# Windowed attention plus a gated FFN on one core: moving one weight load to the sync queue and adding window sums in three steps

## The chip, the core and the metric

The kernel runs on one core of a Trainium2 chip. The core has a matrix engine (TensorE, PE in the profile), a vector engine (VectorE, DVE), a scalar engine (ScalarE, ACT), GpSimd (POOL), and SyncE (SP), which here only issues transfers. Transfers run on 16 DMA engines; those issued by SyncE go through hardware queue q1, those issued by GpSimd through software queue q0. The metric is the device time of one execution in microseconds; less is better.

## The reference

One layer norm feeds an attention over a dilated window and a gated feed-forward network; both results are added to the input. The shapes are: 2048 tokens, 640 features, 32 heads of 20 features, a window of 8 positions that are 2 apart, 1536 hidden features, all in bf16.

```python
def _A_ref(x, wqkv, wo):                       # H = 32, W, dil = 8, 2
    q, k, v = ...                              # x @ wqkv, split into heads
    idx = pos[:, None] - (jnp.arange(W) * dil)[None, :]
    kg, vg = k[:, :, idx_c, :], v[:, :, idx_c, :]
    logits = jnp.einsum("bhsd,bhswd->bhsw", q, kg) * scale
    logits = jnp.where(mask[None, None, :, :], logits, -1e9)   # idx >= 0
    attn = _softmax(logits, axis=-1)           # over the 8 slots of the window
    o = jnp.einsum("bhsw,bhswd->bhsd", attn, vg)
    return o.transpose(...) @ wo
def _B_ref(x, w_gate, w_up, w_down):
    return ((x @ w_gate) * (x @ w_up)) @ w_down

xn = _layernorm(x, axis=-1)
return x + _A_ref(xn, A_wqkv, A_wo) + _B_ref(xn, B_w_gate, B_w_up, B_w_down)
```

## The kernel before

The 2048 tokens are four chunks (`c` = 0 to 3) of 512, and each chunk is four tiles (`ttl`) of 128; `tg` counts the sixteen tiles. A chunk goes through these stages.

- `norm(c, ...)`: VectorE takes the statistics of each tile (`stats`), GpSimd the reciprocal root, VectorE scales (`xn`). For chunk 0 TensorE transposes the tiles. For the later chunks `keep` (line 294) stores the four tiles to `xnD` in DRAM and `turn_all` (line 302) loads them back transposed into `xnT`, both on the sync queue. For those chunks the tile `xn` lies in the buffer ring `pw` of six buffers, which the products of the logits use too, so a product may have to wait until the store of `xn` is through.
- `vproj(c)` and `qk(c)`: projections on TensorE; ScalarE copies them out of PSUM. The values go to DRAM (`vD`), on the sync queue for chunk 0 and on GpSimd's for the others.
- `weights(c)` (line 424): eight products `pw` of `qT` with a shifted `kT` on VectorE, one for each slot of the window. Each group of four is followed by `heads`, 20 matmuls with the constant `Ek` that add up the 20 features of each head (`lps`), and by an exponential on ScalarE into `e`.
- `turned_weights(c)` (line 462): `keep_e` stores `e` to `eD`, and `turn_e` loads it transposed as `eT`, both on the sync queue.
- `attend(c, ttls)` (line 490): once per chunk `normal`, planned as `("a", c)`, which adds up the 8 slots of every head, takes the reciprocal and scales `eT`. Then for each tile, on VectorE: `mix` (the gathered values `v8` times the weights) and three halving additions (`add4`, `add2`, `add1`); the result is stored to `oD` and loaded transposed as `oT`. `v8` has two buffers; the load of the tile after next is issued when a tile is done.
- `glu(c)` (line 558): gate and up matmuls (`psg`, `psu`), copied out by ScalarE, multiplied by VectorE into `hT`.
- `finish(c)` (line 591): for each tile and each half of the output columns 5 matmuls with `wo_perm` and 12 with `wd` into `psf`, then on VectorE the addition of the input tile `xr`, then the store. For a chunk's first tile the last 4 of the 12 come in a unit of their own, since the last `hT` come late.

The weights are loaded once. `load_down` (line 158) loads the output weights `wo_perm` (four DMAs of 200 KB) and the down weights `wd` (one of 1920 KB); `load_ffn` loads gate and up weights (four DMAs of 960 KB). Both are issued on GpSimd's queue, `load_down` behind `load_ffn` and the constants.

The order in which each engine gets its instructions is written out by a small planner when the program is built (`run`, line 197). It keeps a clock for TensorE and one for VectorE, in microseconds of its own. An operation (`op`) has a planned cost and a time from which it may start. At each step the engine that is behind takes an operation: first one from its list of interludes (`burst` for TensorE, which holds `heads`; `quick` for VectorE, which holds `hT`, the mask and the residuals), if one is due, otherwise the next one of its main line (`main` for TensorE, `chain` for VectorE). Entries in `later`, most of them DMA issues, are put out as soon as the slower of the two clocks has reached their due time. What the planner reckons decides only the order on each engine. On the chip each instruction waits for its operands, and an engine never passes an instruction that waits.

In this plan `turn_e` falls due 3.0 after `keep_e`, `eT` counts as there 7.0 after `turn_e`, and `normal` costs 2.8. `heads` counts as ready 0.9 after its fourth product has been planned to end (`LAG` 0.2 and a slack of 0.7). VectorE's chain from line 652 on is: norms of chunks 0 and 1, `weights(0)`, norm of chunk 2, all four tiles of `attend(0)`, `weights(1)`, norm of chunk 3, tiles 4 and 5, `weights(2)`, tiles 6 to 9, `weights(3)`, the rest. TensorE's main line is at lines 678 to 693.

Of the kernel before, what the change touches and what calls it, by code (L numbers as in the profile page):

```python
# [10 lines left out]
F32 = dt.float32  # L11
# [6 lines left out]
def kernel(  # L18
# [139 lines left out]
    def load_down():  # L158
        wo_r = A_wo.rearrange("(h t jl) d -> jl h t d", h=H, t=KT, jl=JL)
        for jl in range(JL):  # L160
            nc.gpsimd.dma_start(out=wo_perm[jl * H : (jl + 1) * H, :, :], in_=wo_r[jl])
        nc.gpsimd.dma_start(out=wd[:], in_=B_w_down.rearrange("(f p) d -> p f d", p=P))

    def warm_up(n):
        wps = ps_log.tile([P, CS], F32, name="wps", tag="lg")
# [60 lines left out]
    def norm(c, group):  # L226
        st = state[c]
        st["xnT"] = None

        def alloc():  # L230
            if st["xnT"] is None:
                st["xnT"] = cpool.tile([P, KT, CS], BF, name="xnT", bufs=3)

        def steps(t0):
            g = {}

            def stats():
                g["mv"] = cpool.tile([P, group, nc.vector.BN_AGGR_DIM], F32, name="mv", bufs=2)
                for k in range(group):
                    x_t = x_tiles[c * CH + t0 + k]  # L240
                    s = cpool.tile([P, 2, nc.vector.BN_STATS_DIM], F32, name="stats")
                    for hf in range(2):
                        nc.vector.bn_stats(s[:, hf, :], x_t[:, hf * N2 : (hf + 1) * N2])  # L243
                    nc.vector.bn_aggr(g["mv"][:, k, :], s[:])
                rstd = cpool.tile([P, group], F32, name="rstd", bufs=2)
                g["rstd"] = rstd
                if c == 0 and t0 < 2:
                    nc.scalar.activation(rstd[:], g["mv"][:, :, 1], ACT.Sqrt, bias=eps[:])
                    return
                nc.gpsimd.tensor_scalar(rstd[:], g["mv"][:, :, 1], EPS, None, op0=ALU.add)  # L250
                nc.gpsimd.tensor_tensor(
                    rstd[:], rstd[:], mhalf[:].to_broadcast([P, group]), ALU.pow
                )

            def stats_after(t):
                if c == 0 and t0 < 2:
                    on("act", ("rstd", c, t0), t + LAG, 0.25)
                    return
                on("pool", ("rstd", c, t0), t + LAG, 0.85)

            op(chain, ("stats", c, t0), stats, 1.12 * group, None, stats_after)

            def scaling(ttl, k):
                def scale_x():
                    if c == 0 and t0 < 2:
                        nc.vector.reciprocal(g["rstd"][:], g["rstd"][:])
                    if c < 1:
                        xn_t = apool.tile([P, D], BF, name="xn_t", tag="o16")
                    else:
                        if ttl == 0:  # L270
                            st["xn"] = apool.tile([P, CH, D], BF, name="xn", tag="pw", bufs=6)
                        xn_t = st["xn"][:, ttl, :]
                    nc.vector.tensor_scalar(
                        xn_t[:], x_tiles[c * CH + ttl][:],
                        scalar1=g["mv"][:, k, 0:1], scalar2=g["rstd"][:, k : k + 1],
                        op0=ALU.subtract, op1=ALU.mult,
                    )
                    st["xn", ttl] = xn_t

                def turn():  # L280
                    alloc()
                    pst = ps_tr.tile([P, KT, P], BF, name="pst", tag="tr")
                    for i in range(KT):
                        nc.tensor.transpose(
                            pst[:, i, :], st["xn", ttl][:, i * P : (i + 1) * P], ident[:]
                        )
                    nc.scalar.copy(st["xnT"][:, :, tcols(ttl)], pst[:])
                    if c == ttl == 0:
                        warm_up(14)

                def turned(t):
                    on("act", ("xnT", c, ttl), t + LAG, 0.7)

                def keep():
                    nc.sync.dma_start(
                        out=xnD[c * CS : (c + 1) * CS, :].rearrange("(t p) d -> p t d", p=P),
                        in_=st["xn"][:],
                    )
                    done["kept", c] = min(clock["pe"], clock["dve"])
                    later.append((turn_all, lambda t=clock["dve"]: t + 4.0))  # L300

                def turn_all():
                    alloc()
                    nc.sync.dma_start_transpose(
                        out=st["xnT"][:],
                        in_=xnD[c * CS : (c + 1) * CS, :].rearrange("m (k p) -> m k p", p=P),
                    )
                    done["stored", c] = min(clock["pe"], clock["dve"])
                    done["turned", c] = min(clock["pe"], clock["dve"])
                    for k in range(CH):  # L310
                        done["xnT", c, k] = done["turned", c] + 8.0

                def scaled(t):
                    if c >= 1:
                        if ttl == CH - 1:
                            later.append((keep, lambda t=t: t))
                        return
                    op(burst, ("turn", c, ttl), turn, 0.3, when(("xn", c, ttl)), turned,
                       ("tr", ("xnT", c, ttl)), 0.7)

                def later_free():
                    old = done.get(("turn", c, ttl - 2), INF) if c < 1 else 0.0
                    return max(done.get(("rstd", c, t0), INF), old if ttl >= 2 else 0.0)

                op(chain, ("xn", c, ttl), scale_x, 0.43 if c or t0 >= 2 else 0.53, later_free, scaled,
                   ("pw", ("stored", c)) if c >= 1 and ttl == 0 else None)

            return [lambda k=k: scaling(t0 + k, k) for k in range(group)]

        if group == 1:  # L330
            for pair in ((0, 1), (2, 3)):
                for f in [steps(t0)[0] for t0 in pair]:
                    f()
        else:
            for t0 in range(0, CH, group):
                for f in steps(t0):
                    f()
# [124 lines left out]
    def turned_weights(c):  # L462
        st = state[c]

        def mask():
            nc.vector.tensor_tensor(
                st["e"][:, :, 0:MC], st["e"][:, :, 0:MC], vmask[:], ALU.mult
            )

        def keep_e():  # L470
            rows = eD[c * 2 * P : (c + 1) * 2 * P, :]
            nc.sync.dma_start(out=rows.rearrange("(g p) t -> p g t", p=P), in_=st["e"][:])
            later.append((turn_e, lambda t=min(clock["pe"], clock["dve"]): t + 3.0))

        def turn_e():
            st["eT"] = apool.tile([P, CH, 2 * P], BF, name="eT")
            rows = eD[c * 2 * P : (c + 1) * 2 * P, :]
            nc.sync.dma_start_transpose(
                out=st["eT"][:], in_=rows.rearrange("r (t p) -> r t p", p=P)
            )  # L480
            done["turned e", c] = min(clock["pe"], clock["dve"])
            done["eT", c] = done["turned e", c] + 7.0

        exps = when(("exp", c, 0), ("exp", c, 1))
        if c == 0:
            op(quick, ("mask", c), mask, 0.1, exps)
            exps = when(("mask", c))
        later.append((keep_e, exps))

    def attend(c, ttls):  # L490
        st = state[c]

        def normal():
            eT = st["eT"][:].rearrange("p t (w h) -> p t w h", h=H)
            rs = apool.tile([P, CH, H], F32, name="rs", bufs=1)
            nc.vector.tensor_reduce(
                rs[:], eT.rearrange("p t w h -> p t h w"), axis=AX.X, op=ALU.add
            )
            nc.vector.reciprocal(rs[:], rs[:])
            nc.vector.tensor_tensor(  # L500
                eT, eT, rs[:, :, None, :].to_broadcast([P, CH, W, H]), ALU.mult
            )

        if ttls[0] == 0:
            op(chain, ("a", c), normal, 2.8, when(("eT", c)))
        for ttl in ttls:
            tg = c * CH + ttl

# [140 lines left out]
    def side(fn):  # L649
        op(chain, ("side", len(chain)), fn, 0.0)  # L650
# [2 lines left out]
    side(load_ffn)  # L653
    norm(1, 4)
    side(constants)
    side(load_down)
    later.append((lambda: load_x(2), when(("v", 0, CH - 1, 1))))
    later.append((lambda: want_v8(0), when(("kept", 1))))
    weights(0)
# [5 lines left out]
    weights(1)  # L665
    turned_weights(1)
    norm(3, 4)
    attend(1, range(2))
    weights(2)
    turned_weights(2)  # L670
    attend(1, range(2, CH))
    attend(2, range(2))
    weights(3)
    turned_weights(3)
    attend(2, range(2, CH))
    attend(3, range(CH))

    vproj(0, range(CH))
# [46 lines left out]
```

## Time and profile before

| | |
|---|---|
| median of 6 runs | 275.41 us |
| lowest and highest run | 273.15 and 280.26 us |
| the profiled execution | 273.56 us, its span 271.6 us |
| DMA in the span | 52.18 MB, mean 192 GB/s |
| share of the 16 DMA engines | q1 52.9%, q0 14.0% |
| chain that ended last | PE 59%, DVE 19%, DMA 15% of the span |
| largest groups on VectorE | `pw` 32 products 46.3 us; `hT` 48 products 19.8 us |

The span runs from the first to the last instruction of the profiled execution, and its own time is 2.0 us longer. Busy times of matmuls are modelled and pipelined, so a row's length holds a little of the next row; starts are the better guide. In the rows of the timelines the columns are start, length, engine, line, operation, output and inputs, size and count, and in brackets the idle time before and what ended it. Rows of "SPq" are DMAs at the time they are issued; a DMA lands later. DMAs on the sync queue are issued in program order, and one that waits holds up those behind it.

### The profile page before, as it was taken

What the parts mean: (1) busy time and instruction counts of PE and PEld (TensorE: products, weight loads), DVE (VectorE), ACT (ScalarE), POOL (GpSimd) and SP (SyncE); (2) the same over time, 40 slices, a digit from 0 to 9 for tenths busy, and PEclk for the clock granted to TensorE, in tenths of its full rate; (3) what the DMA queues carried; (4) which work ended last, traced back from release to release, by engine and by line L of the source; (5) the groups of instructions that cost most, each with busy time, mean ns of one, the idle gap of its engine ahead of it and who ended that gap; (6) DMA issues with size and microseconds to landing.
All of it is one profiled execution on the core that took longest, in us unless ns stands there. A gap on an engine that the chain in (4) does not pass through costs nothing.

```text
span 271.6 us, 4138 instructions
## 1 busy us (share of the span) xinstructions
PE 261.5 (96%) x1607; PEld 144.7 (53%) x1624; DVE 202.1 (74%) x260; ACT 104.1 (38%) x185; POOL 39.2 (14%) x81
## 2 busy tenths in 40 slices
PE   7799999999999799999999999999999999999994
PEld 7554443445546367644444677744446774445773
DVE  4453969479689995499999857999999989821221
ACT  3655564555556000155555610054551005554000
POOL 1528201000302204100000131220000302000100
PEclk9999999999999899999999999999999999999998
DMA  6999999692999935705920998597188499210111
GB/s 187 306 381 389 317 364 189 179 264 53 262 315 295 335 99 150 213 32 161 276 46 2 272 312 174 188 271 171 39 228 250 119 292 283 81 47 2 48 48 48
DMA packets 53554, 52.18 MB, mean 192 GB/s; under 512 B 24754, under 2 KB 50816, under 8 KB 53536
## 3 DMA queue, kind: packets, MB, share of 16 engines
q1 hardware_dynamic: 49920, 38.48, 52.9%
q0 software_dynamic: 3616, 13.46, 14.0%
q8 instruction: 12, 0.20, 0.3%
q14 instruction: 6, 0.05, 0.1%
HBM read 35.39 MB, written 10.90 MB: 170 GB/s over the span
## 4 chain that ended last, share of the span: by engine, by line
PE 59%; DVE 19%; DMA 15%; issue 3%; SPq 1%; POOL 1%; ACT 0%; DVEq 0%; ACTq 0%
PE psu L567 15%; PE psg L567 15%; PE psf L616 14%; PE psf L609 6%; DMA xnD<-xn 5%; DVE pw L432 5%; DMA x_t<-in_A_x_dram 4%; PE psqk L360 4%; PE lps L443 3%; DMA v_929<-vD 3%; DMA xr<-in_A_x_dram 2%; PE psv L386 2%; DVE stats L243 1%; DVE v_407 L511 1%; DVE v_929 L511 1%
## 5 line engine op out<-in xcount | busy, mean ns | idle before, releaser
L567 PE MATMUL psu<-xnT,wu 128*128 128x512 bf16 x240 | 59.7, 379 | 0.0
L567 PE MATMUL psg<-xnT,wg 128*128 128x512 bf16 x228 | 59.0, 379 | 0.6
L616 PE MATMUL psf<-wd,hT 128*128 128x320 bf16 x384 | 57.9, 301 | 0.0
L572 ACT CAST gs<-psg 128x512 bf16<-128x512 f32 x48 | 28.1, 586 | 70.0 <-PE psg L567 50.9
L432 DVE TENSOR_TENSOR pw<-qT,kT 128x2560 bf16<-128x2560 bf16 x32 | 46.3, 1484 | 6.2 <-ACT kT L366 3.7
L616 PEld LDWEIGHTS <-hT 128*128 128x128 bf16 x384 | 37.8, 99 | 15.1 <-DVE hT L577 0.2
L360 PE MATMUL psqk<-xnT,wqkv 128*128 128x512 bf16 x195 | 43.9, 379 | 0.3
L567 PEld LDWEIGHTS <-wu 128*128 128x128 bf16 x240 | 23.3, 98 | 28.7 <-issue 0.8
L567 PEld LDWEIGHTS <-wg 128*128 128x128 bf16 x240 | 23.3, 98 | 28.2 <-issue 0.8
L572 ACT CAST us<-psu 128x512 bf16<-128x512 f32 x48 | 28.1, 586 | 26.1 <-PE psu L567 26.1
L623 DVE TENSOR_TENSOR osb<-psf,xr 128x320 bf16<-128x320 f32 x32 | 15.3, 486 | 25.2 <-PE psf L616 19.3
L577 DVE TENSOR_TENSOR hT<-gs,us 128x512 bf16<-128x512 bf16 x48 | 19.8, 418 | 16.5 <-ACT us L572 16.2
L360 PEld LDWEIGHTS <-wqkv 128*128 128x128 bf16 x200 | 19.4, 98 | 23.7 <-issue 0.8
L609 PE MATMUL psf<-wo_perm,oT 128*128 128x320 bf16 x160 | 27.6, 304 | 0.0
L386 PE MATMUL psv<-wqkv,xnT 128*128 128x320 bf16 x160 | 22.7, 299 | 0.0
L633 POOL DMA_DIRECT2D out_dram<-osb x13 | 7.1, 546 | 102.7 <-DVE osb L623 102.6
L609 PEld LDWEIGHTS <-oT 128*128 128x128 bf16 x160 | 15.7, 99 | 7.7 <-issue 1.3
L243 DVE BATCH_NORM_STATS2 stats<-x_t 128x6 f32<-128x320 bf16 x32 | 13.6, 466 | 7.6 <-DMA x_t<-in_A_x_dram 7.6
L386 PEld LDWEIGHTS <-xnT 128*128 128x128 bf16 x160 | 15.5, 98 | 6.3
L398 POOL DMA_DIRECT2D vD<-v_t x12 | 6.6, 552 | 79.1 <-ACT v_t L392 79.1
L392 ACT CAST v_t<-psv 128x320 bf16<-128x320 f32 x32 | 13.6, 426 | 6.9 <-PE psv L386 6.5
L366 ACT CAST qT<-psqk 128x512 bf16<-128x512 f32 x20 | 11.7, 586 | 10.1 <-PE psqk L360 10.1
(94 smaller groups left out, 194.6 us busy)
## 6 DMA issues: line engine op xcount, KB each, us to landing
x_t<-in_A_x_dram SPq DMA_DIRECT2D x16, 160.0 KB, 5.7
xr<-in_A_x_dram POOLq DMA_DIRECT2D x16, 160.0 KB, 3.9
out_dram<-osb POOLq DMA_DIRECT2D x13, 160.0 KB, 2.8
wg<-in_B_w_gate_dram POOLq DMA_DIRECT2D x2, 960.0 KB, 11.1
wu<-in_B_w_up_dram POOLq DMA_DIRECT2D x2, 960.0 KB, 13.3
xnD<-xn SPq DMA_DIRECT2D x3, 640.0 KB, 3.6
wd<-in_B_w_down_dram POOLq DMA_DIRECT2D x1, 1920.0 KB, 14.9
vD<-v_t POOLq DMA_DIRECT2D x12, 160.0 KB, 4.9
```

Of the source, the lines that this page charges most:

```text
L243: nc.vector.bn_stats(s[:, hf, :], x_t[:, hf * N2 : (hf + 1) * N2])
L360: nc.tensor.matmul(ps[:], lhsT=wqkv[:, i, r * D + j * P : r * D + (j + 1) * P], rhs=st["xnT"][:, i, :], start=(i == 0), stop=(i == KT - 1),)
L366: nc.scalar.copy(dst[:, j, o : o + CS], ps[:])
L386: nc.tensor.matmul(ps[:, 0:N2], lhsT=st["xnT"][:, i, tcols(ttl)], rhs=wqkv[:, i, 2 * D + n0 : 2 * D + n0 + N2], start=(i == 0), stop=(i == ...
L392: nc.scalar.copy(v_t[:].rearrange("p (j h) -> p j h", j=Dh)[:, :, k * HH : (k + 1) * HH], ps[:, 0:N2].rearrange("p (h j) -> p j h", j=Dh),)
L432: nc.vector.tensor_tensor(pt[:], st["qT"][:], st["kT"][:, :, off : off + CS], ALU.mult)
L567: nc.tensor.matmul(ps[:], lhsT=w[:, i, f * P : (f + 1) * P], rhs=st["xnT"][:, i, :], start=(i == 0), stop=(i == KT - 1),)
L572: nc.scalar.copy(s[:], ps[:])
L577: nc.vector.tensor_tensor(h[:], st["gu", 0, f][:], st["gu", 1, f][:], ALU.mult)
L609: nc.tensor.matmul(ps[:, 0:N2], lhsT=st["oT", ttl][:, i, :], rhs=wo_perm[:, i, n0 : n0 + N2], start=(i == 0), stop=False,)
L616: nc.tensor.matmul(ps[:, 0:N2], lhsT=st["hT", f][:, tcols(ttl)], rhs=wd[:, f, n0 : n0 + N2], start=False, stop=(f == FT - 1),)
L623: nc.vector.tensor_tensor(osb[:, n0 : n0 + N2], ps[:, 0:N2], xr[:, n0 : n0 + N2], ALU.add)
```

## The change

`load_down` is issued on the sync queue instead of GpSimd's, right behind the transposing load of chunk 1 (in `turn_all`, when `c == 1`), and no longer from VectorE's planned chain. In `normal` the reduction over the slots becomes three additions in f32 over halves: 8 slots to 4, 4 to 2, 2 to 1. Their scratch tile `s4` takes the single buffer of `e`. The planner's figures change: `turn_e` falls due 2.2 after `keep_e`, `eT` counts as there 7.5 after `turn_e`, `normal` costs 3.4. And one tile of `attend(1)` and one of `attend(2)` move behind the next chunk's `weights`.

```diff
     def load_down():
         wo_r = A_wo.rearrange("(h t jl) d -> jl h t d", h=H, t=KT, jl=JL)
         for jl in range(JL):
-            nc.gpsimd.dma_start(out=wo_perm[jl * H : (jl + 1) * H, :, :], in_=wo_r[jl])
-        nc.gpsimd.dma_start(out=wd[:], in_=B_w_down.rearrange("(f p) d -> p f d", p=P))
+            nc.sync.dma_start(out=wo_perm[jl * H : (jl + 1) * H, :, :], in_=wo_r[jl])
+        nc.sync.dma_start(out=wd[:], in_=B_w_down.rearrange("(f p) d -> p f d", p=P))
...
                     done["stored", c] = min(clock["pe"], clock["dve"])
+                    if c == 1:
+                        load_down()
                     done["turned", c] = min(clock["pe"], clock["dve"])
...
-            later.append((turn_e, lambda t=min(clock["pe"], clock["dve"]): t + 3.0))
+            later.append((turn_e, lambda t=min(clock["pe"], clock["dve"]): t + 2.2))
...
-            done["eT", c] = done["turned e", c] + 7.0
+            done["eT", c] = done["turned e", c] + 7.5
...
             rs = apool.tile([P, CH, H], F32, name="rs", bufs=1)
-            nc.vector.tensor_reduce(
-                rs[:], eT.rearrange("p t w h -> p t h w"), axis=AX.X, op=ALU.add
+            s4 = apool.tile([P, CH, 4, H], F32, name="s4", tag="e", bufs=1)
+            nc.vector.tensor_tensor(s4[:], eT[:, :, 0:4, :], eT[:, :, 4:8, :], ALU.add)
+            nc.vector.tensor_tensor(
+                s4[:, :, 0:2, :], s4[:, :, 0:2, :], s4[:, :, 2:4, :], ALU.add
             )
+            nc.vector.tensor_tensor(rs[:], s4[:, :, 0, :], s4[:, :, 1, :], ALU.add)
...
-            op(chain, ("a", c), normal, 2.8, when(("eT", c)))
+            op(chain, ("a", c), normal, 3.4, when(("eT", c)))
...
-    side(load_down)
...
-    attend(1, range(2))
+    attend(1, range(1))
     weights(2)
     turned_weights(2)
-    attend(1, range(2, CH))
-    attend(2, range(2))
+    attend(1, range(1, CH))
+    attend(2, range(1))
     weights(3)
     turned_weights(3)
-    attend(2, range(2, CH))
+    attend(2, range(1, CH))
     attend(3, range(CH))
```

## The prediction

> **What bounds the kernel now.** I read the page first, then the waits, then TensorE in order of time, then the granted clock, and last VectorE and the queues where TensorE had waited.
>
> ```profile
> span 271.6 us, 4138 instructions
> PE 261.5 (96%) x1607; PEld 144.7 (53%) x1624; DVE 202.1 (74%) x260; ACT 104.1 (38%) x185; POOL 39.2 (14%) x81
> PEclk9999999999999899999999999999999999999998
> ```
>
> TensorE is the bound: 271.6 - 261.5 leaves 10.1 us without a matmul, most of it before the weights arrive and after the last matmul. What can be won inside is small, and it lies where TensorE waits for VectorE or runs at a lower clock (the lone 8 in PEclk).
>
> ```profile
> PE lps L443 <- DVE pw L432: 2.4, 3, 1.0
> ```
> ```profile
> 42.00 1.24 PE L443 MATMUL lps<-pw,Ek 128*32 128x512 bf16 x17 [0.49 <-DVE pw L432]
> ```
> ```profile
> 87.50 0.84 PE L609 MATMUL psf<-wo_perm,oT 128*128 128x320 bf16 x5
> 88.18 1.25 PE L616 MATMUL psf<-wd,hT 128*128 128x320 bf16 x8
> 89.36 0.39 PE L443 MATMUL lps<-pw,Ek 128*32 128x512 bf16 x2
> 90.60 0.38 PE L443 MATMUL lps<-pw,Ek 128*32 128x512 bf16 x1 [0.85 <-DVE pw L432]
> 92.00 1.75 PE L443 MATMUL lps<-pw,Ek 128*32 128x512 bf16 x17 [1.03 <-DVE pw L432]
> ...
> 97.67 0.84 PE L609 MATMUL psf<-wo_perm,oT 128*128 128x320 bf16 x5
> ...
> 100.07 1.26 PE L443 MATMUL lps<-pw,Ek 128*32 128x512 bf16 x20
> ```
> ```profile
> 92.00:93.00 1.00, 1.00 (x16) 0.79 1.07 385
> ...
> 95.00:96.00 1.00, 1.00 (x5) 0.50 1.01 335
> ```
>
> The expensive place is the logits of chunk 1, `heads(1,0)`: TensorE arrives at 89.36, three of its 20 matmuls can run, and the fourth waits for the fourth `pw` product until 92.00. Then the clock is at 0.50 for the 3.4 us from about 92.8 (the columns are busy time, clock, DMA). The wait costs some 2.5 us, the half clock half of 3.4, so 1.7: 4.2 us in one place. A lesser stall, 0.49 us, stands at 42.00.
>
> **Part 1, the load moved.** On GpSimd's queue `load_down` sits behind the gate and up weights:
>
> ```profile
> 25.23 2.34 POOL L161 DMA_DIRECT2D wo_perm<-in_A_wo_dram  x4
> 27.56 1.07 POOL L162 DMA_DIRECT2D wd<-in_B_w_down_dram  x1
> 46.39 0.28 POOL L250 TENSOR_SCALAR rstd<-mv 128x4 f32<-128x4 f32 x1 [17.77 <-DVE mv L244]
> ```
> ```profile
> 22.83 0.40 SPq L295 DMA_DIRECT2D xnD<-xn  x1
> 30.06 0.38 SPq L412 DMA_DIRECT2D v_407<-vD  x1
> 37.23 7.89 SPq L304 DMA_TRANSPOSE xnT<-xnD  x1
> 46.69 0.38 SPq L472 DMA_DIRECT2D eD<-e  x1
> 49.83 0.38 SPq L295 DMA_DIRECT2D xnD<-xn  x1
> 50.30 1.90 SPq L478 DMA_TRANSPOSE eT<-eD  x1
> ```
> ```profile
> q0 software_dynamic: 965, 3.93, 68.7%
> ```
> ```profile
> q0 software_dynamic: 393, 1.57, 89.6%
> q1 hardware_dynamic: 209, 0.26, 14.2%
> ```
> ```profile
> 33.33 1.48 DVE L432 TENSOR_TENSOR pw<-qT,kT 128x2560 bf16<-128x2560 bf16 x1
> 37.31 1.49 DVE L432 TENSOR_TENSOR pw<-qT,kT 128x2560 bf16<-128x2560 bf16 x1 [2.50 <-DMA xnD<-xn]
> ```
>
> By 29 us q0 has moved 3.93 MB (window 14 to 29), just the four 960 KB gate and up loads; so from 29 on its traffic is this load alone. From 30 to 36 it leaves sync's queue 0.26 MB, and chunk 1's `xnD` store, issued at 22.83, lands only at 37.2, where its transpose starts. That store holds a `pw` buffer, and VectorE stands 2.50 us for it.
>
> Without the load, the some 0.34 MB still missing at 30 (0.26, and a little to 37.2) go at the rate of sync's queue alone:
>
> ```profile
> DMA packets 2030, 2.36 MB, mean 295 GB/s; under 512 B 187, under 2 KB 2030, under 8 KB 2030
> ```
>
> (window 4 to 12). That is 1.2 us: landing near 31.2, bounds 30 and 37.2. The 2.50 us wait goes; its product ran 37.31 to 38.7 and the two after it to 41.9, all now 2.5 earlier, ahead of TensorE's arrival at 41.12. Gain on TensorE 0.49 us, bounds 0 and 0.49.
>
> The price is the new place. Five issues at 0.4 us are 2 us on SP; POOL is freed 3.4 us, worth nothing, as it idles until 46.39. Behind them on SP and in its ring is `e`'s store (46.69). In ring order, at 295 GB/s: `v_407` (1.31 MB, 4.4 us) to 35.6, the transpose (0.66 MB, 2.2) to 37.8, wo and wd (4 x 200 + 1920 KB = 2.79 MB, 9.4) to 47.2.
>
> ```profile
> eD<-e SPq DMA_DIRECT2D x1, 256.0 KB, 2.1
> eT<-eD SPq DMA_TRANSPOSE x1, 4.2
> ```
>
> The `e` store then lands near 49.3 instead of 48.8, and `eT` near 53.5. Its user `a(0)` stands behind the last `hT` (below), so 2.3 us of cover are left. The weights themselves are wanted at 87.50: 40 us of cover.
>
> **Part 2, three additions for the reduction.**
>
> ```profile
> 55.92 0.42 DVE L577 TENSOR_TENSOR hT<-gs,us 128x512 bf16<-128x512 bf16 x1 [1.64 <-ACT us L572]
> 56.27 1.88 DVE L496 TENSOR_REDUCE rs<-eT 128x128 f32<-128x1024 bf16 x1
> ...
> 60.42 2.83 DVE L511 TENSOR_TENSOR v_407<-v_407,eT 128x5120 bf16<-128x5120 bf16 x1
> ...
> 74.13 2.83 DVE L511 TENSOR_TENSOR v_855<-v_855,eT 128x5120 bf16<-128x5120 bf16 x1 [2.32 <-DMA v_855<-vD]
> ...
> 86.26 11.30 DVE L432 TENSOR_TENSOR pw<-qT,kT 128x2560 bf16<-128x2560 bf16 x8
> ```
> ```profile
> 46.50 0.17 DVE L466 TENSOR_TENSOR e<-e,vmask 128x32 bf16<-128x32 bf16 x1
> ```
> ```profile
> L623 DVE TENSOR_TENSOR osb<-psf,xr 128x320 bf16<-128x320 f32 x32 | 15.3, 486 | 25.2 <-PE psf L616 19.3
> ```
>
> Removed: 1.88 us. Added: 512, 256 and 128 elements, f32 out. Bounds: at the reduction's own 1.83 ns an element, 896 elements make 1.64 us; at the rate of the all-bf16 `hT` (0.42 for 512, then about 0.27 and 0.2) 0.9 us. The nearest row with an f32 operand is `osb`: 486 ns for 320. With some 0.14 us fixed (the 32-element row takes 0.17) that is 1.08 ns an element, and 0.69 + 0.42 + 0.28 = 1.39, with two more gaps of 0.03: 0.43 saved per chunk, bounds 0.2 and 0.95. All of it lies in VectorE's chain `a(0)`, four tiles, `pw(1,..)`. `s4` takes the slot of `e`: it waits for the `e` store, which `eT` already awaited, and the next `e` waits for additions that stand ahead of its own `pw` products on VectorE: nothing.
>
> `a(0)` starts when the last `hT` of chunk 0 is done, paced by TensorE: 56.27 - 0.49. The chain is then 0.49 + 0.43 = 0.92 earlier, if `v_855`'s load (a 2.32 us wait) shifts along, as it starts when the first tile's buffer is free. Fourth `pw`: 86.26 + 4 x 1.41 = 91.9, now 91.0. Eighth: 97.6, now 96.6.
>
> **Part 3, the planner's figures.** They move instructions and cost none. Following its clock through the code, `turn_e` falls due at 45.16 + 2.2 and goes out at 47.65 instead of 48.47, ahead of chunk 2's `xnD` store on SP, no longer behind it (49.83 before 50.30). `eT` counts as there at 55.15 (55.47 before), `a(0)` takes 3.4 for 2.8, so the chain is planned 0.30 later. `heads(1,0)` was planned ready at 87.58 with TensorE free at 87.76; now 87.88 is too late, and one more finish unit of 13 matmuls goes first. That is the main effect: TensorE works 1.8 us (87.50 to 89.36) where it stood. By the same clock `heads(1,1)` keeps its place.
>
> Moving one tile's attention behind `weights(2)` and `weights(3)` moves equal VectorE work; `heads(2)` and `heads(3)` come 5.7 us sooner (2.83 and three additions of 1.5, 0.8, 0.5), tiles 5 to 7 and 9 to 11 finish at the old end. It might free the small stall here:
>
> ```profile
> 184.75 1.76 PE L443 MATMUL lps<-pw,Ek 128*32 128x512 bf16 x20
> ```
>
> 0.5 us over the 1.26 of 100.07. VectorE still waits for a residual's `xr` before it, and planned order moves with it: I take 0, bounds -0.5 and +0.5.
>
> **The sum.** TensorE reaches finish at 87.0, runs two units to 90.6, waits for the fourth `pw` to 91.1, ends heads at 92.1 (17 matmuls, 1.0), then 8 matmuls (1.1) and 17 (2.4 by 97.67 to 100.07) to 95.6; `heads(1,1)` now waits for the eighth `pw` to 96.7 and ends at 97.7, against 101.3. What is late next is that wait, 1.0 us. Gain 3.6 us, the 0.49 within it. The profiled execution took 273.56: it becomes 270.0. It stood 1.85 under the median of the six runs (275.41); I add half of that, since this stall and its clock window can differ among them: 270.9.
>
> **Rivals.**
> *The half clock stays* (0.15). The waits are still 0.3 and 1.0 us, 5 us apart. If they suffice, 1.7 us are lost again: gain 1.9, 272.6. Against it, a longer stop passed at full clock (the clock's slices there are all 9):
>
> ```profile
> 10.71 0.45 PE L284 MATMUL pst<-ident,xn_t 128*128 128x128 bf16 x5 [1.38 <-DVE xn_t L273]
> ```
>
> The Trainium skill, "TensorE: Matmul & The Clock Gate", part 1, has the clock halve after an idle window of about 3.4 us and stay so for at least one. The 3.4 us at 0.50 agree; the stop ahead of it held three matmuls, so idle need not be total. By that rule waits of 1 us stay free and the time is the 270.9 above.
>
> *The chain gains nothing* (0.12): `v_855` waits longer by what is won. Fourth and eighth `pw` at 91.9 and 97.6, `heads(1,1)` ends at 98.7: gain 2.6, 271.9.
>
> *The change does nothing* (0.05): the heads meet the same wait. 273.56 + 0.9, 274.5.
>
> *Slower: the load holds up `e`* (0.10). All rests on 2.79 MB passing the ring in 9.4 us. The cover is 2.3 us; each microsecond beyond moves both `pw` and TensorE. With the half clock back (1.7) the gain is eaten at 3.6 - 1.7 = 1.9 us beyond, so from 13.6 us for the load (205 GB/s); 7 us beyond turns 3.6 into a loss of 5.1: 273.56 + 5.1 + 0.9, 279.6.
> The Trainium skill, "DMA: Bandwidth & Descriptors", on queues, rings and completion order, has descriptors taken in ring order and an engine alternating between rows. By that rule the store gets no share until the load is through, as reckoned; before, q0 and q1 shared.
>
> **How the numbers follow.** The forecast has 0.58. Its own range is 268.5 (all 4.2 + 0.49 + 0.5 won against 273.56, 268.4) to 272.5. With the half clock and the pinned chain it is 268.5 to 274.5, which leaves the last two rivals and the tail out. One per cent, about what a measurement here can tell, is 2.75 us. Faster by more: 0.62 (the forecast, and a part of the pinned chain); within: 0.28; slower: 0.10.
>
> **What would show it.** `xnD` landing near 31 and no wait before the sixth `pw`; wo and wd landing by 48, `eT` issued near 49.5 ahead of `xnD`; `rs` chain 3.7 us instead of 4.15; 26 finish matmuls before `heads(1,0)`; no 0.5 in the clock near 93. An `eT` issued after 53, or a clock of 0.5 after `heads(1,1)`, would make it wrong.

## The result and the profile after

| | before | after |
|---|---|---|
| median of the runs | 274.98 us (20 runs, 271.8 to 280.26) | 267.73 us (10 runs, 267.19 to 268.93) |
| the profiled execution, its span | 273.56, 271.6 us | 267.41, 265.7 us |

The ratio of the times is 0.9775, with a 95% interval from 0.9743 to 0.9807: the kernel is 1.9 to 2.6% faster. The median, 267.73 us, lies 0.8 us below the low end of the predicted range; the 275.41 us from which the prediction started, times the ratio, make 269.2 us, which lies in it. The spread of the runs shrank too, from 8.5 us to 1.7 us, and that turned out to be the better clue to what the change does than anything in the two profiles. A ratio leaves out the runs that are more than 1.5% above the fastest of their own kernel, which for the kernel before are up to 14 of 23, though the spread of its runs is part of what the change removes, so the medians of all runs stand beside the ratios and lie further apart.

The page of the kernel after, in the lines that answer to those shown of before:

```profile
span 265.7 us, 4139 instructions
PE 260.1 (98%) x1607; PEld 145.4 (55%) x1624; DVE 200.7 (76%) x268; ACT 104.0 (39%) x185; POOL 35.6 (13%) x76
PEclk9999999999999999999999999999999999999999
```

TensorE now has 5.6 us without a matmul, where it had 10.1, and no slice with a lower clock. In order of time, TensorE at the three places where it had waited (columns as before: start, length, instruction):

```profile
25.35 1.24 PE L572 MATMUL psg<-xnT,wg 128*128 128x512 bf16 x4
...
40.77 1.26 PE L445 MATMUL lps<-pw,Ek 128*32 128x512 bf16 x20
41.96 1.25 PE L572 MATMUL psu<-xnT,wu 128*128 128x512 bf16 x5
...
86.29 0.84 PE L614 MATMUL psf<-wo_perm,oT 128*128 128x320 bf16 x5
86.97 1.25 PE L621 MATMUL psf<-wd,hT 128*128 128x320 bf16 x8
88.06 0.84 PE L614 MATMUL psf<-wo_perm,oT 128*128 128x320 bf16 x5
88.74 1.25 PE L621 MATMUL psf<-wd,hT 128*128 128x320 bf16 x8
89.92 1.69 PE L445 MATMUL lps<-pw,Ek 128*32 128x512 bf16 x20
91.54 1.26 PE L621 MATMUL psf<-wd,hT 128*128 128x320 bf16 x8
...
97.35 1.26 PE L445 MATMUL lps<-pw,Ek 128*32 128x512 bf16 x20
...
107.79 1.24 PE L572 MATMUL psg<-xnT,wg 128*128 128x512 bf16 x4
...
172.16 1.26 PE L445 MATMUL lps<-pw,Ek 128*32 128x512 bf16 x20
```

Read by starts. `heads(0,1)`, at 40.77, runs all 20 matmuls without a stop. Before `heads(1,0)`, at 89.92, there are 26 matmuls of `finish` and not 13; the group takes 1.62 us to the next start where an undisturbed one takes 1.20, so a wait of 0.4 us is left of the old 2.5. `heads(1,1)`, at 97.35, doesn't wait, and neither does `heads(3,0)` at 172.16.

Laid beside the starts of the same instructions before, the kernel after is ahead by 0.34 us where `glu(0)` begins (25.69 against 25.35), by 1.21 where `finish(0)` begins (87.50 against 86.29), by 5.03 where `glu(1)` begins (112.82 against 107.79), and by 5.57 at `finish(3)` (249.43 against 243.86). So in these two profiles 0.87 us come from `heads(0,1)`, 3.82 from the two `heads` of chunk 1 with the half clock behind them, 0.5 from `heads(3,0)`, and the rest of the 5.9 us of span from the start and the tail. On that reading the load's move is worth less than 1 us. The experiments show that this does not hold for the other executions of the kernel before.

VectorE and the sync queue after:

```profile
54.72 0.43 DVE L582 TENSOR_TENSOR hT<-gs,us 128x512 bf16<-128x512 bf16 x1 [1.64 <-ACT us L577]
55.06 0.69 DVE L499 TENSOR_TENSOR s_789<-eT 128x512 f32<-128x512 bf16 x1
55.78 0.42 DVE L500 TENSOR_TENSOR s_789<-s_789 128x256 f32<-128x256 f32 x1
56.24 0.29 DVE L503 TENSOR_TENSOR rs<-s_789 128x128 f32<-128x128 f32 x1
...
58.81 2.83 DVE L516 TENSOR_TENSOR v_402<-v_402,eT 128x5120 bf16<-128x5120 bf16 x1
...
72.94 2.83 DVE L516 TENSOR_TENSOR v_858<-v_858,eT 128x5120 bf16<-128x5120 bf16 x1 [2.65 <-DMA v_858<-vD]
...
84.63 9.89 DVE L434 TENSOR_TENSOR pw<-qT,kT 128x2560 bf16<-128x2560 bf16 x7
94.44 0.88 DVE L628 TENSOR_TENSOR osb<-psf,xr 128x320 bf16<-128x320 f32 x2
95.24 1.48 DVE L434 TENSOR_TENSOR pw<-qT,kT 128x2560 bf16<-128x2560 bf16 x1
```
```profile
22.78 0.39 SPq L295 DMA_DIRECT2D xnD<-xn  x1
30.40 0.38 SPq L414 DMA_DIRECT2D v_402<-vD  x1
32.06 4.82 SPq L304 DMA_TRANSPOSE xnT<-xnD  x1
...
40.22 0.60 SPq L162 DMA_DIRECT2D wd<-in_B_w_down_dram  x1
...
50.97 1.27 SPq L480 DMA_TRANSPOSE eT<-eD  x1
```

And the DMAs after in two windows (columns: size, and time from issue to landing), 30 to 36 and 40 to 56 us:

```profile
v_402<-vD SPq DMA_DIRECT2D x1, 1280.0 KB, 6.2
xnT<-xnD SPq DMA_TRANSPOSE x1, 9.2
```
```profile
wd<-in_B_w_down_dram SPq DMA_DIRECT2D x1, 1920.0 KB, 10.1
eT<-eD SPq DMA_TRANSPOSE x1, 3.3
```

The `xnD` store has landed at 32.06, where its transposing load starts. The transposed chunk is there at 41.3 (32.06 + 9.2), the weights at 50.3 (40.22 + 10.1), `eT` at 54.3 (50.97 + 3.3). The first of the three additions begins at 55.06, directly behind the last `hT`: 0.8 us of cover are left.

### The profile page after: what moved, and what is told of

Same layout as the page of the kernel before. It is cut to its first block, busy times and chain, and to the rows that moved or that the text cites. A ratio compares the mean times of both kernels' runs of the same rounds, so it can differ in the third digit from the quotient of the medians.

```text
span 265.7 us, 4139 instructions
## 1 busy us (share of the span) xinstructions
PE 260.1 (98%) x1607; PEld 145.4 (55%) x1624; DVE 200.7 (76%) x268; ACT 104.0 (39%) x185; POOL 35.6 (13%) x76
## 4 chain that ended last, share of the span: by engine, by line
PE 81%; DVE 10%; DMA 4%; issue 1%; SPq 1%; POOL 0%; ACT 0%; ACTq 0%
PE psu L572 20%; PE psg L572 19%; PE psf L621 19%; PE psqk L362 8%; PE psf L614 8%; PE lps L445 4%; PE psv L388 3%; DMA v_942<-vD 3%; DVE pw L434 2%; DMA x_t<-in_A_x_dram 1%; DVE v_942 L516 1%; DVE v_402 L516 1%; DVE v_719 L516 1%; DVE v_942 L532 1%; DVE v_402 L532 1%
## 5 line engine op out<-in xcount | busy, mean ns | idle before, releaser
L614 PE MATMUL psf<-wo_perm,oT 128*128 128x320 bf16 x160 | 27.0, 299 | 0.0
## 6 DMA issues: line engine op xcount, KB each, us to landing
wd<-in_B_w_down_dram SPq DMA_DIRECT2D x1, 1920.0 KB, 10.1
```

The lines of the kernel that those rows point to most:

```text
L614: nc.tensor.matmul(ps[:, 0:N2], lhsT=st["oT", ttl][:, i, :], rhs=wo_perm[:, i, n0 : n0 + N2], start=(i == 0), stop=False,)
```

## The experiments

All runs but the second profile of the kernel before are timed beside the kernel before, whose medians in the three series were 275.04, 274.52 and 274.99 us and whose lowest runs were 269.89, 271.35 and 270.14 us. The three series ran on different chips, so a difference of less than about 1 us between medians of different series is not shown to be real.

### One part alone on the kernel before

The load alone:

```diff
-            nc.gpsimd.dma_start(out=wo_perm[jl * H : (jl + 1) * H, :, :], in_=wo_r[jl])
-        nc.gpsimd.dma_start(out=wd[:], in_=B_w_down.rearrange("(f p) d -> p f d", p=P))
+            nc.sync.dma_start(out=wo_perm[jl * H : (jl + 1) * H, :, :], in_=wo_r[jl])
+        nc.sync.dma_start(out=wd[:], in_=B_w_down.rearrange("(f p) d -> p f d", p=P))
...
+                    if c == 1:
+                        load_down()
...
-    side(load_down)
```

> The kernel before with the load moved alone. Theory (the place of the heads of chunk 1 on TensorE carries most of the gain): the stall at the second heads of chunk 0 goes (0.86 us by the starts of its rows), heads(1,0) still stands after 13 finish matmuls and waits some 2 us for its fourth product, the clock halves behind it as before; 0.5 to 1.3 us faster, ratio 0.995 to 0.998. Rival (the earlier loads pull the whole chain of VectorE forward and carry the gain): 4 us or more faster, ratio 0.985 or less, and no half clock near 92 us.

Measured: 270.57 us (270.22 to 271.44), ratio 0.9883 [0.9844, 0.9922]. By medians 4.5 us are gone, by the ratio 1.2%, or 3.2 us; with them goes the spread: 1.2 us where the kernel before has 7.3 in this series. The ratio lies between the range of the theory and that of the rival. The wait at `heads(1,0)` is still there, as its TensorE timeline shows:

```profile
89.56 0.38 PE L445 MATMUL lps<-pw,Ek 128*32 128x512 bf16 x1 [0.87 <-DVE pw L434]
90.96 1.24 PE L445 MATMUL lps<-pw,Ek 128*32 128x512 bf16 x17 [1.03 <-DVE pw L434]
92.13 0.85 PE L611 MATMUL psf<-wo_perm,oT 128*128 128x320 bf16 x5
```

It is as long as in the first profile of the kernel before, so a VectorE chain that comes earlier, the rival's way, is not what carries the gain. Only the half clock behind the wait is missing here, which makes 1.6 us against that profile (23.72 us from `finish(0)` to `glu(1)`, where it has 25.32). A load that moves no instruction near `heads(1,0)` gains more than half of the whole, and the theory of the prediction, in which the planner's figures carry most of it, does not fit this.

The planner's figures alone:

```diff
-            later.append((turn_e, lambda t=min(clock["pe"], clock["dve"]): t + 3.0))
+            later.append((turn_e, lambda t=min(clock["pe"], clock["dve"]): t + 2.2))
...
-            done["eT", c] = done["turned e", c] + 7.0
+            done["eT", c] = done["turned e", c] + 7.5
...
-            op(chain, ("a", c), normal, 2.8, when(("eT", c)))
+            op(chain, ("a", c), normal, 3.4, when(("eT", c)))
```

> The kernel before with the planner's three figures alone (2.2, 7.5, 3.4). Theory: heads(1,0) stands after 26 finish matmuls and heads(1,1) after a unit more of 17, VectorE's chain is as late as before, so TensorE waits 0.5 to 1 us instead of 2.5 and the clock stays full: 3 to 4 us faster, ratio 0.986 to 0.989, with runs that lie closer together. Rival (the load carries it): within 0.5 us of before.

Measured: 276.54 us, from 269.57 to 279.32 in six runs, too far apart for a ratio. Its lowest run is a little lower than any of the kernel before in this series (269.89), its highest is higher than all of them (277.2). The 3 to 4 us of the theory are not there, and runs that lie closer together are not either. In its profile `finish(0)` takes 21.80 us to the start of `glu(1)` (25.32 before), so the new place does what was said of it; but up to `finish(0)` it needs 65.89 us from the start of `glu(0)`, where before needs 61.81. Something that differs by 4 us between these two profiles hides the gain.

The three additions alone:

```diff
-            nc.vector.tensor_reduce(
-                rs[:], eT.rearrange("p t w h -> p t h w"), axis=AX.X, op=ALU.add
-            )
+            s4 = apool.tile([P, CH, 4, H], F32, name="s4", tag="e", bufs=1)
+            nc.vector.tensor_tensor(s4[:], eT[:, :, 0:4, :], eT[:, :, 4:8, :], ALU.add)
+            nc.vector.tensor_tensor(
+                s4[:, :, 0:2, :], s4[:, :, 0:2, :], s4[:, :, 2:4, :], ALU.add
+            )
+            nc.vector.tensor_tensor(rs[:], s4[:, :, 0, :], s4[:, :, 1, :], ALU.add)
```

> The kernel before with the three additions alone. Theory: the sums and the scaling take 3.75 us instead of 4.15, heads(1,0) waits 2.1 us instead of 2.5; 0.4 us faster, at most 2.1 if the shorter wait spares the half clock in most runs; ratio 0.992 to 0.999. Rival (the cheaper additions carry the gain): 3 us or more.

Measured: 274.44 us (270.28 to 280.88), ratio 0.9972 [0.9911, 1.0034]: not to be told from no change.

The order of `attend` alone:

```diff
-    attend(1, range(2))
+    attend(1, range(1))
     weights(2)
     turned_weights(2)
-    attend(1, range(2, CH))
-    attend(2, range(2))
+    attend(1, range(1, CH))
+    attend(2, range(1))
     weights(3)
     turned_weights(3)
-    attend(2, range(2, CH))
+    attend(2, range(1, CH))
```

> The kernel before with the new order of attend and weights alone. Theory: the small stall at heads(3,0) (0.5 us) goes and nothing else; 0 to 0.5 us faster, ratio 0.998 to 1.0. Rival: heads(2,0), now planned 7.6 earlier on TensorE, waits for VectorE, whose products come only 5.7 earlier: 1 to 2 us slower.

Measured: 278.58 us, ratio 1.0152 [1.0094, 1.021]: alone it is slower by 3.5 us in the median. Its profile accounts for about 0.9 us of that. `heads(3,0)` is planned inside `finish(1)` there and still waits, and the next stretches are 0.4 and 0.5 us longer than before:

```profile
177.99 1.24 PE L443 MATMUL lps<-pw,Ek 128*32 128x512 bf16 x17 [0.38 <-DVE pw L432]
```

A part of the other 2.6 us is half clock: all six of its runs show a mean granted clock of 0.986 to 0.994, where 10 of the 17 of the kernel before beside it show 0.997 or more. A spell of 3.4 us at half clock, which is what its profile shows twice, takes 0.006 off that mean and costs 1.7 us. Why every run has such a spell with this order stays open.

### The kernel after with one part undone

Each edit is the reverse of the corresponding one above; in the third the cost of 3.4 is kept, so that the order of all other instructions stays.

Load back on GpSimd's queue, at its old place:

> The changed kernel with the load back on GpSimd's queue. Theory: it loses the stall at the second heads of chunk 0 (0.86 us) and VectorE's chain comes 0.9 later to heads(1,0), where TensorE waits 1 us instead of 0.4: 1 to 1.7 us slower than the changed kernel, ratio to before 0.981 to 0.984. Rival (the load carries the gain): ratio 0.99 or more.

Measured: 274.27 us (one run of 460.78 stands far off), ratio 0.9914 [0.9867, 0.9961]: by medians 6.5 us of the gain are lost, by the ratios 1.4%, or 3.8 us. This is the rival, not the theory.

Old figures:

> The changed kernel with the planner's old figures (3.0, 7.0, 2.8). Theory: heads(1,0) goes back behind 13 finish matmuls and waits 2 us or more, with the half clock behind it in many runs: 2 to 4 us of the gain are lost, ratio to before 0.987 to 0.995, and runs that lie further apart. Rival (the chain of VectorE, not the place, carries it): ratio 0.98 or less.

Measured: 271.25 us (269.26 to 273.22), ratio 0.9917 [0.9875, 0.9958]: 3.5 us lost, as expected, but not by the half clock, which its profile does not show.

Reduction back:

> The changed kernel with the reduction in place of the three additions, planned cost still 3.4. Theory: the chain comes 0.4 us later to heads(1,0), which waits 0.8 instead of 0.4: 0.3 to 0.5 us slower than the changed kernel, ratio to before 0.979 to 0.981. Rival (the additions carry more): 1 us or more slower.

Measured: 268.68 us (one run of 557.26 stands far off), ratio 0.9823 [0.9771, 0.9875]: 1.0 us lost by medians, more than the 0.3 to 0.5 of the theory, though the intervals of this ratio and of the kernel after overlap. The profiled execution, at 271.6 us, is a poor example of its runs: a value load came late on VectorE, and `heads(3,0)` had to wait for it.

```profile
151.87 2.83 DVE L513 TENSOR_TENSOR v<-v,eT 128x5120 bf16<-128x5120 bf16 x1 [4.27 <-DMA v<-vD]
```

Old order of `attend`:

> The changed kernel with the old order of attend and weights. Theory: heads(3,0), planned 2.6 later than in the kernel before with these figures, meets its products in time, so the stall of 0.5 us does not come back or only in part: 0 to 0.5 us slower than the changed kernel, ratio to before 0.978 to 0.980. Rival (the order is worth more than the 0.5 us that one stall shows): 1 us or more slower.

Measured: 268.40 us (267.66 to 269.51), ratio 0.9824 [0.9778, 0.987]: 0.7 us lost by medians, with runs that overlap those of the kernel after. Its profile has no wait at `heads(3,0)` either. That does not show that the figures remove this wait: with the figures alone, in the old order, `heads(3,0)` waits 0.71 us in the profile, and with the old figures in the new order 0.34. It differs from profile to profile, and no run here ties it to one part.

So by medians the load carries most of the gain. The next series asks by which way: through the `pw` buffer that the store of `xn` holds, or through something else that the load disturbs.

### What the load does on GpSimd's queue

The load on the sync queue at its old point in the plan, which puts it in the ring directly behind the `xnD` store and ahead of the transposing load:

```diff
-            nc.gpsimd.dma_start(out=wo_perm[jl * H : (jl + 1) * H, :, :], in_=wo_r[jl])
-        nc.gpsimd.dma_start(out=wd[:], in_=B_w_down.rearrange("(f p) d -> p f d", p=P))
+            nc.sync.dma_start(out=wo_perm[jl * H : (jl + 1) * H, :, :], in_=wo_r[jl])
+        nc.sync.dma_start(out=wd[:], in_=B_w_down.rearrange("(f p) d -> p f d", p=P))
```

> The kernel before with the load issued on the sync queue at its old point, so right behind chunk 1's store of xn in the same ring. Theory (the load must not share the DMA engines with that store; its later place is not needed): the store lands by 32 us, the products of chunk 0 do not wait, TensorE reaches finish(0) near 86.4; within 1.5 us of the load moved alone, ratio 0.984 to 0.993. Rival (it has to come behind the transposing load): the gathered values and the transpose come some 9 us later, a(0) starts late and the gain is lost; ratio 0.997 or more.

Measured: 270.84 us (270.09 to 272.45), ratio 0.9935 [0.9894, 0.9977]: by medians 4.2 us, within 0.3 us of what the load's move alone gave; the ratio lies a little above the expected range and clear of the rival's 0.997. The sync queue shows the load right behind the store, and the store's time from issue to landing:

```profile
22.21 0.40 SPq L295 DMA_DIRECT2D xnD<-xn  x1
22.66 3.67 SPq L161 DMA_DIRECT2D wo_perm<-in_A_wo_dram  x4
...
32.99 11.90 SPq L304 DMA_TRANSPOSE xnT<-xnD  x1
```
```profile
xnD<-xn SPq DMA_DIRECT2D x1, 640.0 KB, 9.3
```

The store lands at 31.5 (22.21 + 9.3). Whether the weights stand behind the transposing load or ahead of it makes no difference that shows in the medians; that they leave GpSimd's queue and stand behind the store does.

The load untouched on GpSimd's queue, but chunk 1's `xn` in a buffer of the value tiles, so that its store no longer holds one of the six `pw` buffers:

```diff
-                            st["xn"] = apool.tile([P, CH, D], BF, name="xn", tag="pw", bufs=6)
+                            if c == 1:
+                                xv = apool.tile([P, W, D], BF, name="xv", tag="v8")
+                                st["xn"] = xv[:, 0:CH, :]
+                            else:
+                                st["xn"] = apool.tile([P, CH, D], BF, name="xn", tag="pw", bufs=6)
```

> The kernel before, load on GpSimd's queue as it was, but chunk 1's xn in a buffer of the gathered values, which is free then, instead of one of the products' six. Theory (the load costs by holding the store, and the store by holding a product's buffer): the store lands as late as before (37 to 41 us), yet no product waits for it, TensorE reaches finish(0) near 86.4 instead of 87.5 to 92.5: 3 to 5 us faster, ratio 0.984 to 0.99, runs within 3 us of each other. Rival (the late loads of chunk 1 hold something else as well): ratio 0.995 or more, finish(0) later than 88 us.

Measured: 270.56 us (270.0 to 272.96), ratio 0.9949 [0.9907, 0.9991]: by medians 4.4 us again, with the load where it was. The ratio is above the expected range and within 0.0001 of the rival's 0.995; the median, the spread of 3.0 us and `finish(0)`, which starts at 86.97 and not later than 88, are the theory's. The sync queue and TensorE:

```profile
42.00 3.62 SPq L308 DMA_TRANSPOSE xnT<-xnD  x1
```
```profile
41.44 1.26 PE L447 MATMUL lps<-pw,Ek 128*32 128x512 bf16 x20
```

The store lands at 42.0, later than in any other profile, and nothing waits: `heads(0,1)` runs its 20 matmuls at 41.44 in one go. The store is as late as ever, only the buffer has changed, and the wait is gone: the late store holds up chunk 0 through the buffer that it occupies.

The kernel before, unchanged, once more:

> The kernel before once more, for a second profile. Theory (the stall at the second heads of chunk 0 differs from run to run and the first profile had a mild one): the store of xn lands between 37 and 41 us, the product waits 2.5 to 5.7 us, and TensorE reaches finish(0) at 87.5 plus what the store is later than 37.2, with the half clock added if the stop is long. Rival (it is always the 2.5 us of the first profile): finish(0) at 87.5 within 0.5 us.

Measured: 275.97 us in the profiled execution. VectorE, then TensorE, then the queues from 30 to 36 us (columns: packets, MB, share of the 16 engines):

```profile
39.77 1.49 DVE L432 TENSOR_TENSOR pw<-qT,kT 128x2560 bf16<-128x2560 bf16 x1 [5.50 <-DMA xnD<-xn]
```
```profile
40.57 0.39 PE L443 MATMUL lps<-pw,Ek 128*32 128x512 bf16 x1
41.32 0.38 PE L443 MATMUL lps<-pw,Ek 128*32 128x512 bf16 x1 [0.35 <-DVE pw L432]
43.05 0.38 PE L443 MATMUL lps<-pw,Ek 128*32 128x512 bf16 x1 [1.36 <-DVE pw L432]
44.46 2.29 PE L443 MATMUL lps<-pw,Ek 128*32 128x512 bf16 x17 [1.03 <-DVE pw L432]
46.68 1.57 PE L567 MATMUL psu<-xnT,wu 128*128 128x512 bf16 x5
```
```profile
q0 software_dynamic: 380, 1.53, 88.1%
q1 hardware_dynamic: 229, 0.27, 16.2%
```

The same program, and the wait is 5.50 us and not 2.50. The store lands at 39.7 instead of 37.2, the last product is late by as much, and TensorE loses the time of three waits and then that of a half clock: the last 17 matmuls take 2.2 us to the next start, where they take 1.2 in the profile of the load alone, above. `finish(0)` starts at 91.33, 3.8 us later than in the first profile. The half clock at this place is not in the profile on which the prediction rests.

The rest of the change with the load on GpSimd's queue and the buffer of the run before last:

> All of the change except the moved load, which stays on GpSimd's queue, and chunk 1's xn in the buffer of the gathered values. Theory: the buffer does all that the moved load did, so the time is the changed kernel's within 1 us: ratio to before 0.975 to 0.982. Rival (the moved load does more than free the buffer): ratio 0.985 or more.

Measured: 268.69 us (267.6 to 270.35), ratio 0.9862 [0.9793, 0.9931]: within 1.0 us of the kernel after by medians, without the move of the load. The ratio lies above the theory's range, in the rival's, so a smaller advantage of the moved load is not excluded. Up to `finish(1)` the two profiles agree within 0.1 us; from there to `glu(3)` this one is 1.5 us longer, with a wait of 0.45 us for a late `oT` and one of 0.48 us at `heads(3,0)`.

The stretches of TensorE in the profiles, by starts; every value is the difference of two starts in its timeline:

| profile | wait of `pw` for `xnD` | start of `glu(0)` to `finish(0)` | `finish(0)` to `glu(1)` |
|---|---|---|---|
| before, first profile | 2.50 | 61.81 | 25.32 |
| before, second profile | 5.50 | 66.18 | 23.86 |
| figures alone | 4.95 | 65.89 | 21.80 |
| additions alone | 5.07 | 66.01 | 23.36 |
| order alone | 4.16 | 65.10 | 25.25 |
| after, load back | 5.74 | 66.58 | 21.39 |
| after | none | 60.94 | 21.50 |
| load alone | none | 60.95 | 23.72 |
| load on sync, old point | none | 60.94 | 25.37 |
| own buffer | none | 60.95 | 23.58 |
| own buffer and the rest | none | 60.95 | 21.52 |

Without the wait, the first stretch is the same to 0.01 us in all profiles (60.95 also in the kernel after with the old figures, the old order or the reduction). With it, it is 0.87 us longer in one and 4.2 to 5.6 us longer in five.

## Why the prediction was half right

**Part 1, the load: the mechanism was right, its size was not.** The store was to land near 31.2 and landed at 32.1; the `pw` wait went. The term that failed is "Gain on TensorE 0.49 us, bounds 0 and 0.49". It measured 0.87 us even in the profile it was read from, because the idle column is cut short by modelled lengths of matmuls that overlap the gap; by starts the stretch is 61.81 against 60.94. And in five other profiles with the load on GpSimd's queue it is 4.2 to 5.6 us. The three runs that take the wait away alone gain 4.2 to 4.5 us by medians and 0.5 to 1.2%, or 1.4 to 3.2 us, by the ratios, which leave out the longest of the runs before. The upper bound was the size of one stall in one execution, taken for the size in all, and no half clock was reckoned behind this stall, where all five of those profiles have one. The runs' granted clocks give an estimate of its part: of 62 runs of the kernel before in the three series (without one of 557.62 us) 31 have a mean clock of 0.997 or more and a median of 273.4 us, the other 31 a median of 276.9; the load alone has 270.6. So some 2.8 us are to be won even where no spell of half clock fell.

The new place of the load cost nothing, but the cover was thinner than reckoned: the weights came at 50.3 and not 47.2, `eT` at 54.3 and not 53.5, and 0.8 us of cover were left of 2.3. The load itself took 9.0 us (41.3 to 50.3), near the 9.4 reckoned. Most of the delay was ahead of it, in the transposing load: from the landing of `v_402` at 36.6 it took 4.7 us and not 2.2.

**Part 2, the additions: right.** They take 0.69, 0.42 and 0.29 us, and from the first one to the first `mix` it is 3.75 us (55.06 to 58.81), where it was 4.15. The Trainium skill, "VectorE: DVE Perf Modes", section on the TRN2 errata, gives an fp32 addition of N elements (N + 151) / 0.96 ns; that is 0.69, 0.42 and 0.29 us, so the rule and the trace agree, also for the first addition, whose inputs are bf16. The chain was not pinned by the value load: its wait grew from 2.32 to 2.65 us, and the products of chunk 1 still began 1.63 us earlier (84.63 against 86.26). With the reduction put back, 1.0 us is lost by medians, which is not clear of the spread; done alone they gain nothing that can be told.

**Part 3, the figures: the place right, the weight and one detail wrong.** `heads(1,0)` did go behind 26 matmuls, and the half clock did not come. The detail that failed is "`heads(1,1)` keeps its place" and so "waits for the eighth `pw`" for 1.0 us. In the plan two residual additions now fall between the seventh and the eighth product (94.44 in VectorE's timeline), and `heads(1,1)` moved behind one more unit of 17 matmuls, to 97.35, without a wait. The step that failed is "That is the main effect". In the profiles the new place saves some 2 us against the old (21.4 to 22.1 against 23.1 to 23.9), 3.8 where the half clock followed; the load's 4.2 to 5.6 is more, and without the load's move the figures show in no median. With it they are worth 3.5 by medians.

**The order of `attend`** was put at 0 within 0.5 us. In the kernel after it is worth 0.7 us by medians, within the spread of the runs; that it removes the 0.5 us at `heads(3,0)` is not shown. That it loses 3.5 us alone was not foreseen.

**The sum and the median.** Against the profiled execution 270.0 us were predicted and 267.41 measured. Of the 2.6 us, 0.4 are the size of the first stall, 0.7 the two `heads` of chunk 1, 0.5 `heads(3,0)`, and the rest start, tail and what lies around the span, which the prediction did not touch. Then 0.9 us were added, half of what the profiled run lay under the median, "since this stall and its clock window can differ among them". The thought was right and was given to the wrong stall: what differs most from run to run is the wait for the store with the half clock behind it, and the change removes it. Nearly all of the 1.85 was to be won: the median of the kernel after lies only 0.3 us above its profiled execution.

**The rivals.** The half clock stayed away behind `heads(1,0)`, as it did there in the five other profiles with its new place. The chain was not pinned, and the change did something. The rival on the slow side, the load that holds up `e`, was nearer than its 10% say: 0.8 us of cover.

What stays open: why the store lands at 37.2 in one execution and between 39.1 and 40.6 in five others, what decides the wait at `heads(3,0)`, and why the order alone brings a half clock in every run.

## What to carry to other kernels

A DMA that holds a buffer of a ring is on the path of everyone who takes the next buffer: when a store shares the engines with a large load of another queue, put the load behind it in the same queue, or give the store a buffer of its own. When the runs of a kernel spread far more than its stalls in one profile can explain, take a second profile before pricing a stall. Price a stall by the difference of starts on the engine, not by the idle column, where matmul lengths overlap.

## What the runs showed of the hardware

The share that a queue gets depends much on who else is busy. With the load on GpSimd's queue, sync's queue moved 0.27 MB of 1.80 from 30 to 36 us, at 229 packets against 380 larger ones, and the 640 KB store took 17.2 us from issue to landing (22.48 to 39.70); the same load issued directly behind the store in one queue left it at 9.3 us (22.21 to 31.5, the load on the sync queue at its old point). The Trainium skill, "DMA: Bandwidth & Descriptors", section on queues, rings and completion order, has each DMA engine take turns between queues packet by packet; the packet counts are nearer to each other than the bytes, which agrees with it in kind.

The half clock is not a matter of the length of the stop alone. The load on the sync queue at its old point stops at `heads(1,0)` as the load alone does, within 0.02 us, and is followed by 3.4 us at half clock:

```profile
89.54 0.38 PE L443 MATMUL lps<-pw,Ek 128*32 128x512 bf16 x1 [0.89 <-DVE pw L432]
90.94 1.46 PE L443 MATMUL lps<-pw,Ek 128*32 128x512 bf16 x17 [1.03 <-DVE pw L432]
92.34 1.51 PE L609 MATMUL psf<-wo_perm,oT 128*128 128x320 bf16 x5
```

Five matmuls of `psf` take 1.51 us here and 0.85 in the other run. The old place of `heads(1,0)` led to the half clock in 3 of 8 profiles, the stall at `heads(0,1)` in 5 of the 6 that have the load on GpSimd's queue and the shared buffer: in the five whose product waited 4.2 us or more, and not in the one where it waited 2.5. The Trainium skill, "TensorE: Matmul & The Clock Gate", part 1, has a window of about 3.4 us that runs freely and halves the clock after an idle one; a free window would explain that the same stop is caught or missed by chance, which no run here tests, and the length of the spell agrees. But the stops here, 2.6 us at `heads(1,0)`, are shorter than such a window and have matmuls in them.
